# Three small moves in a one-core transformer-block kernel: a GpSimd row copy, two table tests, and the router's row

## The chip, the cores and the metric

The kernel runs on one core of a Trainium2 chip. A core has engines with an instruction queue each, and each queue runs in order: PE (TensorE, matrix products), ACT (ScalarE), DVE (VectorE), POOL (GpSimd) and SP (SyncE, which here only issues DMA transfers). A queue whose first instruction waits for a semaphore holds back everything behind it. The metric is the device time of one execution in microseconds (us); lower is better.

## The reference

One block on x of 2048 tokens by 512 features. A condition vector c gives six rows (shift, scale and gate, twice) through `silu(c) @ w_mod`. The first half is a Fourier mixing layer with DFT matrices that are handed in as inputs, the second a feed-forward network on the one token that a router picks.

```python
mod = (silu(c) @ w_mod).reshape(1, 6, 1, 512)
sa, ca, ga, sb, cb, gb = (mod[:, i] for i in range(6))
h = layernorm(x) * (1 + ca) + sa
a, b = h @ hid_re.T, h @ hid_im.T            # 512 x 512
x = x + ga * (seq_re @ a - seq_im @ b)       # 2048 x 2048 each
h = layernorm(x) * (1 + cb) + sb
r = h @ w_r                                  # a score for each token
k = argmax(r)                                # one token of 2048
y = (silu(h[k] @ w_gate) * (h[k] @ w_up)) @ w_down
x = x + gb * (h + scatter(k, y * sigmoid(r[k])))
```

## The kernel before

The two sequence matrices hold 32 MB, far more than the transform needs when they really are a cosine and a sine table. The kernel therefore takes a short path, `folded`, that computes the transform from a few columns of them, and on the way it reads all 32 MB and tests that each number is the one that the symmetry foresees. If a test fails, a flag sends the program to a long path, `general`, which does not run with these inputs.

**The tests.** The 32 MB come as 32 tiles of 128 x 2048 (1 MB each; `tst`), loaded by SP (line 600) into a ring of slots F1, R2, F2, R4, R0, R1 and R3. A slot first holds something else (R0 to R4 the weights `wm` that make the six rows, F1 and F2 the normalised input `n` of class 1) and takes its next tile when the one in it has been tested. `run_test(k)` puts the next k tests into the program at the place where it is called: six of the tests (numbers 12, 14, 16, 19, 24 and 27) are counted on VectorE (line 619, 2.3 us each), all others summed on ScalarE (line 631, 2.0 us each). A call thus decides where a test stands among an engine's other work, and with it when its slot comes free, and so where the next load can be issued by SP, which works through its list in the order of the program.

**The front.** The tokens stand in two classes of eight tiles of 128 tokens, each class in two quads: (class, quad) is (1, 0), (1, 1), (0, 0), (0, 1). The first three quads get their mean and variance by VectorE (`bn_stats`, lines 241 and 242), then four small instructions on GpSimd (lines 245 to 248) make the factor `rsa` and the shift `nma`, and ScalarE normalises the four tiles into `n` (line 276). The quad (0, 1) gets its sums from ScalarE (line 259 on) and its last steps from GpSimd (lines 269 to 272, `sst`). VectorE adds and subtracts mirrored tiles (`p`, lines 696 to 700), multiplies by the row `ca` (706) and folds (712 to 716) into `z` and `odd`. PE turns `odd` into `so` (line 792, four PSUM banks); ScalarE copies these to `xo` (line 813). PE also makes the rows of the condition: `pm_ca`, `pm_sa` (line 142), then `pq_b` and `pq_g` (line 160), whose weights lie in R3, R2, R4 and R0.

A row of 4.5 KB, `lone`, is loaded by SP into the slot `early`; its last 129 numbers are copied to `lrow` by GpSimd (line 590). `lrow` is first read in the even sequence, by the small product `sz<-lrow,lz`.

**The middle.** PE forms `h` from `xo` (line 894) for the first two pairs of token tiles, then the even sequence `st`, `sz` (line 792), then `h` of the other six pairs. VectorE adds `h` to x (282), takes the mean (290), the router's score (313), the output (334, 338); ScalarE squares (297) and makes the gains (327); GpSimd makes the factor `rs` (308, 309). SP stores each pair (353) and loads the network's weights `w_gate`, `w_up` and `w_down` (360, 363) into slots that tests and tables leave.

**The end.** `route` finds the token of the highest score: VectorE reduces to `mp`, PE turns it into one row `prow`, a copy of half of it goes to `row`, and VectorE finds the maximum (391 to 396). PE spreads the result (`pb`, `pw`, `px`), and `ffn` runs: `pg`, `pu` (467), `pd` (518), then the sum `fr` and its store of one row of the output (547), which must come after the stores of the tiles that hold this row. `keep_warm(n)` issues n products of zeros on PE; the list `WARM` has their numbers at four places of `route`, of which the first stands ahead of `prow` and the second between `prow` and `pb`.

Of the kernel before, what the change touches and what calls it, by code (L numbers as in the profile page):

```python
# [10 lines left out]
AF = mybir.ActivationFunctionType  # L11
# [3 lines left out]
P = 128  # L15
# [16 lines left out]
RD = float(D) ** 0.5  # L32
BIG = 4096.0
TOL = 2.0**-33
WARM = (44, 11, 6, 10)
EW = 4 * P + 2
SLOT = 4 * EW
SMALL = 3 * NT + NTEST + 1 + 21
# [13 lines left out]
class Path:  # L52
# [318 lines left out]
    def route(self, fill=iter(()), verdict=lambda: None):  # L371
        nc, one = self.nc, self.one
        self.keep_warm(WARM[0])
        mp = one.tile([P, 2], F32, name="mp")
        nc.gpsimd.tensor_tensor(self.nm, self.mean, self.rs, op=ALU.mult)
        nc.vector.tensor_mul(self.r, self.r, self.rs)
        nc.vector.tensor_reduce(mp[:, 0:1], self.r, axis=AX.X, op=ALU.max)
        eq = one.tile([P, NT], F32, name="eq")
        nc.vector.scalar_tensor_tensor(eq, self.r, mp[:, 0:1], self.nt, op0=ALU.is_equal, op1=ALU.mult)
        nc.vector.tensor_reduce(mp[:, 1:2], eq, axis=AX.X, op=ALU.max)  # L380
        next(fill, None)
        prow = self.ps("prow")
        for k in range(2):
            nc.tensor.matmul(
                prow[0:1, k * P : (k + 1) * P], mp[:, k : k + 1], self.ident, start=True, stop=True
            )
        self.keep_warm(WARM[1])
        row = one.tile([1, P], F32, name="row")
        nc.scalar.activation(row, prow[0:1, P : 2 * P], AF.Copy)
        fin = one.tile([1, 2], F32, name="fin")  # L390
        nc.vector.tensor_reduce(fin[:, 0:1], prow[0:1, 0:P], axis=AX.X, op=ALU.max)
        row2 = one.tile([1, P], F32, name="row2")
        nc.vector.scalar_tensor_tensor(
            row2, prow[0:1, 0:P], fin[:, 0:1], row, op0=ALU.is_equal, op1=ALU.mult
        )
        nc.vector.tensor_reduce(fin[:, 1:2], row2, axis=AX.X, op=ALU.max)
        next(fill, None)
        pb = self.ps("pb")
        nc.tensor.matmul(pb[:, 0:2], self.ones[0:1, :], fin, start=True, stop=True)
        self.keep_warm(WARM[2])  # L400
        bst = one.tile([P, 2], F32, name="bst")
        nc.vector.tensor_copy(bst, pb[:, 0:2])
        sel = one.tile([P, 5], F32, name="sel")
        for i, tab in enumerate((self.tid, self.rs, self.nm, self.rid, self.ones[:, 0:NT])):
            hit = one.tile([P, NT], F32, name=f"hit{i}")
            nc.vector.scalar_tensor_tensor(
                hit, self.nt, bst[:, 1:2], tab, op0=ALU.is_equal, op1=ALU.mult, accum_out=sel[:, i : i + 1]
            )
        pw = self.ps("pw")
        nc.tensor.matmul(pw[:, 0:4], self.ones, sel[:, 0:4], start=True, stop=True)  # L410
        self.keep_warm(WARM[3])
        ti = one.tile([1, 2], I32, name="ti")
        nc.vector.tensor_copy(ti, pw[0:1, 0:4:3])
        tj = nc.vector.value_load(ti[0:1, 0:1], min_val=0, max_val=NT - 1)
        xw = self.scrap("xw", "o")
        nc.vector.tensor_copy(xw, self.xall[:, bass.ds(tj, 1), :])
        px = self.ps("px")

        for k in range(ND):
            nc.tensor.matmul(px[:, k : k + 1], xw[:, k:D:ND], sel[:, 1:2], start=True, stop=True)  # L420
        win = one.tile([P, 2], F32, name="win")
        nc.vector.tensor_copy(win, pw[:, 1:3])
        verdict()
        xs = one.tile([P, ND], F32, name="xs")
        nc.vector.scalar_tensor_tensor(
            xs, px[:, 0:ND], win[:, 1:2], self.cbs[:, 0, :], op0=ALU.add, op1=ALU.mult
        )
        nc.vector.tensor_add(xs, xs, self.cbs[:, 1, :])
        self.xw, self.sel, self.win, self.bst, self.ti = xw, sel, win, bst, ti
        return xs  # L430
# [128 lines left out]
class Folded(Path):  # L559
# [26 lines left out]
    def load_lone(self):  # L586
        t = self.early[0:1, 4 * P :][:, 0 : 8 * P + ZC]
        self.nc.sync.dma_start(t, self.io["lone"])
        self.erow, self.v1 = t[:, 0 : 4 * P], t[:, 4 * P : 8 * P]
        self.nc.gpsimd.tensor_copy(self.lrow, t[:, 8 * P :])  # L590

    def free(self, *names):

# [314 lines left out]
    def verdict(self):  # L908
        nc, one, tot = self.nc, self.one, self.tot
        self.bad = one.tile([1, 1], I32, name="bad")  # L910
        nc.vector.tensor_reduce(tot[:, 0:1], self.esum, axis=AX.X, op=ALU.add)
        nc.vector.tensor_tensor(tot[:, 2:3], tot[:, 0:1], tot[:, 1:2], op=ALU.is_le)
        nc.vector.tensor_reduce(tot[:, 3:4], self.cnt, axis=AX.X, op=ALU.add)
        nc.vector.scalar_tensor_tensor(
            tot[:, 2:3], tot[:, 3:4], 2048.0 * len(COUNTED), tot[:, 2:3], op0=ALU.is_equal, op1=ALU.mult
        )
        self.pf = pf = self.ps("pf", "acc")
        nc.tensor.matmul(pf[0:1, 0:1], tot[:, 2:3], self.ones[:, 0:1], start=True, stop=True)
# [5 lines left out]
def folded(ctx, tc, io):  # L924
    p = Folded(ctx, tc, io)
    nc = p.nc
# [24 lines left out]
    def mirror(*at):  # L951
        pm[at] = p.mirror(*at, n[at])
# [20 lines left out]
    sums = p.statistics(0, 1, p.scalar_sums)  # L973
    stats = p.statistics(0, 0)
    last = p.scalar_statistics(*sums)
    two = p.mod_pair(wcb, wga, "b")
    p.load_wt(("R1", "R3"))
    n[0, 0] = p.normal(0, 0, stats)
# [20 lines left out]
    p.gb = p.spread_exit(p.mod_spread(other, 1, "gb"), "gb")  # L999
    for i, t in enumerate((p.cb1, p.sb)):  # L1000
        p.mod_b_columns(i, t)
    p.run_test(3)
    mirror(0, 1)
    fold(0, 1)
    p.shift_row(sa)
    p.odd_products(0, 1)
    p.run_test(1)
    p.hidden_sines(ga)
    p.hidden_turned()
    p.lone_row(n[0, 0])  # L1010
    for _ in p.odd_exits():
        pass
# [54 lines left out]
    gains(1)  # L1067
    p.run_test(2)
    p.verdict_small()
    tests = {2: 3, 3: 2, 4: 3, 5: 2, 6: 1}  # L1070
    weights = {2: 1, 3: 1, 4: 2, 5: 2, 6: 3}
    for k in range(2, late):
        begin(k)
# [98 lines left out]
@with_exitstack  # L1172
def adaln_fnet_mod_kernel(ctx: ExitStack, tc: tile.TileContext, io):
    with ExitStack() as fast:
        bad = folded(fast, tc, io)
    with tc.If(bad > 0):
        with ExitStack() as slow:
            general(slow, tc, io)
# [172 lines left out]
```

## Time and profile before

| | |
|---|---|
| time, median of 3 runs | 173.5 us (172.93 to 173.74) |
| the profiled execution: its time, its span | 172.23 us, 170.4 us |
| granted clock of PE, mean | 0.928 |
| busy: PE, DVE, ACT, POOL | 145.0, 122.2, 115.3, 29.9 us |
| moved by DMA | 62.40 MB, mean 366 GB/s |

The span runs from the first to the last instruction of one profiled execution; the time of that execution is 1.8 us longer. Times in the rows below are us from the start of the span. In the rows of the timeline the first column is the start, the second the duration (of several merged instructions where `xN` is above 1), then engine, line, operation, what is written and what is read, and in brackets the idle time of the engine before it and who ended it.

### The profile page before, as it was taken

The page shows a single profiled execution, that of the slowest core. Times are in us where ns is not written, and L with a number is a line of the kernel's source. Part 1 is how long each engine was busy: PE and PEld are TensorE (multiplying, and loading weights), DVE is VectorE, ACT ScalarE, POOL GpSimd, SP SyncE. Part 2 cuts the span into 40 slices and gives each one's busy share as a digit, 9 for nine tenths or more (in the row PEclk, how much of TensorE's full clock was granted, in tenths as well). Part 3 has the DMA queues.
Part 4 walks back from the last instruction along what each step waited for, and adds up shares of the span by engine and source line. Part 5 has one row for each costly group of instructions (what it writes and reads, how often), then busy time and mean ns, then how long its engine had stood idle before and what let it go on. Part 6 is the DMA issues. An engine that isn't in the chain of part 4 may idle for free.

```text
span 170.4 us, 2139 instructions
## 1 busy us (share of the span) xinstructions
PE 145.0 (85%) x680; PEld 69.2 (41%) x680; DVE 122.2 (72%) x256; ACT 115.3 (68%) x189; POOL 29.9 (18%) x67
## 2 busy tenths in 40 slices
PE   7999800599999942999999999999999999689970
PEld 3554300222233211444555444444444455365860
DVE  0680039997999999958779139999999973649250
ACT  3000099987969999999799999999987359400100
POOL 6000440087000002000259103042020301000000
PEclk9999965579999995799999999999999999996999
DMA  4999999501999999999999999999999999999800
GB/s 135 431 414 440 418 421 410 240 0 42 419 413 427 419 411 421 421 408 429 429 421 417 415 431 347 430 423 413 431 417 425 419 420 425 423 425 422 352 34 10
DMA packets 10108, 62.40 MB, mean 366 GB/s; under 512 B 1637, under 2 KB 1641, under 8 KB 4330
## 3 DMA queue, kind: packets, MB, share of 16 engines
q1 hardware_dynamic: 9938, 62.20, 88.8%
q8 instruction: 7, 0.11, 0.3%
q14 instruction: 11, 0.09, 0.1%
q10 hardware_dynamic: 152, 0.00, 0.1%
HBM read 57.99 MB, written 4.20 MB: 365 GB/s over the span
## 4 chain that ended last, share of the span: by engine, by line
PE 38%; DVE 28%; issue 14%; ACT 12%; POOL 5%; DVEq 1%; POOLq 0%; ACTq 0%
PE h L894 13%; ACT tst L631 5%; PE so L792 5%; DVE o L338 4%; DVE tst L619 4%; DVE xall L282 4%; DVE o L334 4%; PE sz L792 4%; DVE tv L313 4%; ACT n L276 3%; PE st L792 3%; PE pg L467 3%; PE pd L518 2%; PE pu L467 2%; POOL rsa L246 2%
## 5 line engine op out<-in xcount | busy, mean ns | idle before, releaser
L631 ACT ACTIVATE tst<-tst,small_in 128x2048 f32<-128x2048 f32 (+1 forms) x27 | 52.0, 1929 | 0.0
L792 PE MATMUL so<-eo,odd 128*128 128x512 f32 (+1 forms) x40 | 21.7, 676 | 10.8 <-DVE odd L716 10.8
L125 PE MATMUL warm<-zb 128*128 128x384 bf16 x132 | 24.9, 348 | 1.1 <-DVE zb L92 1.1
L894 PE MATMUL h<-wc,xo 128*128 128x512 f32 x32 | 16.8, 652 | 5.5 <-ACT xo L813 5.5
L276 ACT ACTIVATE n<-xall,nma,rsa 128x512 f32<-128x512 f32 x12 | 8.8, 802 | 17.5 <-POOL nma L248 17.5
L125 PEld LDWEIGHTS <-zb 128*128 128x128 bf16 x132 | 13.4, 104 | 12.2 <-issue 4.3
L792 PEld LDWEIGHTS so<-eo,odd 128*128 128x128 f32 (+1 forms) x40 | 6.6, 188 | 25.1 <-issue 13.2
L282 DVE SCALAR_TENSOR_TENSOR xall<-xall,h 128x512 f32<-128x512 f32 x16 | 10.5, 682 | 8.7 <-PE h L894 8.7
L297 ACT ACTIVATE jsq<-xall,mean 128x512 bf16<-128x512 f32 x16 | 11.5, 720 | 7.3 <-DVE mean L290 7.0
L619 DVE TENSOR_SCALAR_CACHE_REDUCE tst<-tst,small_in 128x2048 bf16<-128x2048 f32 x6 | 14.0, 2342 | 0.6 <-DMA tst<-in_tst 0.6
L308 POOL TENSOR_SCALAR rs<-ssq 128x2 f32<-128x2 f32 x8 | 3.3, 411 | 59.4 <-ACT jsq L297 59.4
L334 DVE SCALAR_TENSOR_TENSOR o<-xall,mean,n 128x512 f32<-128x512 f32 x16 | 12.0, 747 | 0.9 <-ACT n L327 0.9
L338 DVE SCALAR_TENSOR_TENSOR o<-o,mean,sb 128x512 f32<-128x512 f32 x16 | 12.0, 750 | 0.5
L313 DVE SCALAR_TENSOR_TENSOR tv<-xall,mean,vr 128x512 bf16<-128x512 f32 x16 | 12.0, 751 | 0.5
L699 DVE TENSOR_TENSOR p<-n 128x1024 f32<-128x1024 f32 x3 | 3.6, 1212 | 12.1 <-ACT n L276 12.1
L894 PEld LDWEIGHTS h<-wc,xo 128*128 128x128 f32 x32 | 6.5, 207 | 13.7 <-ACT xo L813 6.9
L894 PE MATMUL h<-wc,xe 128*128 128x512 f32 x24 | 11.3, 592 | 0.0
L327 ACT ACTIVATE n<-cb,rs 128x512 f32<-128x512 f32 x16 | 10.6, 707 | 0.1
L479 ACT ACTIVATE g<-pg 128x256 f32<-128x256 f32 (+1 forms) x2 | 0.7, 358 | 12.2 <-DVE o L334 9.6
L241 DVE BATCH_NORM_STATS2 st<-xall 128x6 f32<-128x512 f32 x12 | 8.0, 667 | 0.0
L309 POOL TENSOR_TENSOR rs<-rs,nhalf 128x2 f32<-128x2 f32 x8 | 7.5, 942 | 0.7
L894 PE MATMUL h<-wp,xo 128*128 128x512 f32 x16 | 7.5, 592 | 0.0
(210 smaller groups left out, 238.6 us busy)
## 6 DMA issues: line engine op xcount, KB each, us to landing
tst<-in_tst SPq DMA_DIRECT2D x32, 1024.0 KB, 10.7
wm<-in_wm SPq DMA_DIRECT2D x6, 1024.0 KB, 15.6
out<-o SPq DMA_DIRECT2D x8, 512.0 KB, 11.3
w_gate<-in_w_gate SPq DMA_DIRECT2D x4, 896.0 KB, 16.4
w_up<-in_w_up SPq DMA_DIRECT2D x4, 896.0 KB, 14.4
w_down<-in_w_down SPq DMA_DIRECT2D x3, 1024.0 KB, 16.2
xall<-in_x SPq DMA_DIRECT2D x1, 2048.0 KB, 14.3
wt<-in_wt SPq DMA_DIRECT2D x2, 1024.0 KB, 4.7
```

Source lines behind the costliest of these rows:

```text
L125: self.nc.tensor.matmul(dst, self.zb[:, 0:P], self.zb, start=True, stop=True)
L276: self.nc.scalar.activation(dst, src, AF.Identity, scale=rs[:, i : i + 1], bias=nm[:, i : i + 1])
L282: self.nc.vector.scalar_tensor_tensor(x, x, 1.0, y, op0=ALU.mult, op1=ALU.add, accum_out=self.sums[:, j : j + 1])
L297: self.nc.scalar.activation(junk, self.xall[:, j, :], AF.Square, bias=self.mean[:, j : j + 1], accum_out=self.ssq[:, j : j + 1],)
L313: self.nc.vector.scalar_tensor_tensor(junk, self.xall[:, j, :], self.mean[:, j : j + 1], self.vr, op0=ALU.add, op1=ALU.mult, accum_out=sel ...
L327: self.nc.scalar.activation(w[:, i, :], self.G, AF.Identity, scale=self.rs[:, j : j + 1], bias=1.0)
L334: self.nc.vector.scalar_tensor_tensor(o[:, i, :], self.xall[:, j, :], nm, w[:, i, :], op0=ALU.add, op1=ALU.mult)
L338: self.nc.vector.scalar_tensor_tensor(o[:, i, :], o[:, i, :], nm, self.sg, op0=ALU.subtract, op1=ALU.add)
L619: self.nc.vector.tensor_scalar(t.bitcast(BF16)[:, 0:2048], t, self.nref[:, i : i + 1], None, op0=ALU.is_equal, op1=ALU.add, accum_out=self ...
L631: self.nc.scalar.activation(v, v, AF.Abs, bias=self.nref[:, acc : acc + 1], accum_out=self.esum[:, acc : acc + 1])
L792: self.nc.tensor.matmul(dst, a, b, start=first and i == 0, stop=last and i == len(ops) - 1)
L894: self.nc.tensor.matmul(bank, src[:, part, dt, b, :], w[:, dt, :], start=n == 0, stop=n == 3)
```

## The change

GpSimd's copy into `lrow` leaves the function that loads the row and stands now behind the last input statistics. The third test of the call `run_test(3)` moves out, so that the tests from number 4 on come one place later each; the call `run_test(1)` that stood ahead of the sine matrices comes behind them; and the number is made up for at the stage of pair 2, which runs four tests instead of three. Since a test's number decides its engine, the six counted ones move along VectorE's list too. The router's `row` is copied by VectorE instead of ScalarE. The first two calls of `keep_warm` in `route` issue five products fewer each.

```diff
-WARM = (44, 11, 6, 10)
+WARM = (39, 6, 6, 10)
...
         row = one.tile([1, P], F32, name="row")
-        nc.scalar.activation(row, prow[0:1, P : 2 * P], AF.Copy)
+        nc.vector.tensor_copy(row, prow[0:1, P : 2 * P])
...
         self.erow, self.v1 = t[:, 0 : 4 * P], t[:, 4 * P : 8 * P]
-        self.nc.gpsimd.tensor_copy(self.lrow, t[:, 8 * P :])
+        self.late_row = t[:, 8 * P :]
...
     last = p.scalar_statistics(*sums)
+    nc.gpsimd.tensor_copy(p.lrow, p.late_row)
...
-    p.run_test(3)
+    p.run_test(2)
     mirror(0, 1)
     fold(0, 1)
     p.shift_row(sa)
     p.odd_products(0, 1)
-    p.run_test(1)
     p.hidden_sines(ga)
     p.hidden_turned()
+    p.run_test(1)
     p.lone_row(n[0, 0])
...
-    tests = {2: 3, 3: 2, 4: 3, 5: 2, 6: 1}
+    tests = {2: 4, 3: 2, 4: 3, 5: 2, 6: 1}
```

GpSimd's list in the front of the program, before; the first `rsa` and `nma` are those of quad (1, 0), the second those of (1, 1):

```order
L584 MEMSET early 1x128 x4
L590 COPY lrow<-early 1x129
L245 TENSOR_SCALAR rsa_211<-mv_202 128x4
L246 TENSOR_TENSOR rsa_211<-rsa_211,nhalf 128x4
L247 TENSOR_TENSOR nma_212<-mv_202,rsa_211 128x4
L248 TENSOR_SCALAR nma_212<-nma_212 128x4
L245 TENSOR_SCALAR rsa_232<-mv_223 128x4
```

and after, from the third statistics on (their first line is the quad (0, 0), `sst` is (0, 1)):

```order
L248 TENSOR_SCALAR nma_232<-nma_232 128x4
L245 TENSOR_SCALAR rsa_335<-mv_326 128x4
L246 TENSOR_TENSOR rsa_335<-rsa_335,nhalf 128x4
L247 TENSOR_TENSOR nma_336<-mv_326,rsa_335 128x4
L248 TENSOR_SCALAR nma_336<-nma_336 128x4
L269 TENSOR_SCALAR sst_306<-sst_305 128x4
L270 TENSOR_TENSOR sst_306<-sst_306,nhalf 128x4
L271 TENSOR_SCALAR sst_306<-sst_306 128x4
L272 TENSOR_TENSOR sst_307<-sst_304,sst_306 128x4
L976 COPY lrow<-early 1x129
L878 MEMSET eh 1x2x512
```

The copy was the first instruction of GpSimd to read something loaded, ahead of all statistics; now all sixteen instructions of the statistics stand ahead of it.

ScalarE's list between the row `gb` and the first `xo`, before:

```order
L182 ACTIVATE gb<-pm_gb 128x512
L631 ACTIVATE tst_424,esum<-tst_424,small_in 128x2048
L631 ACTIVATE tst_426,esum<-tst_426,small_in 128x2048
L631 ACTIVATE tst_428,esum<-tst_428,small_in 128x2048
L631 ACTIVATE tst_431,esum<-tst_431,small_in 128x2048
L868 ACTIVATE wn<-wp,sgn 128x512
L869 ACTIVATE wn<-wp 128x512
L813 ACTIVATE xo<-so_295 128x512
```

and after:

```order
L182 ACTIVATE gb<-pm_gb 128x512
L631 ACTIVATE tst_424,esum<-tst_424,small_in 128x2048
L631 ACTIVATE tst_426,esum<-tst_426,small_in 128x2048
L868 ACTIVATE wn<-wp,sgn 128x512
L869 ACTIVATE wn<-wp 128x512
L631 ACTIVATE tst_428,esum<-tst_428,small_in 128x2048
L813 ACTIVATE xo<-so_294 128x512
```

Four tests stood ahead of the first `xo`, three do now, and one of these three stands behind the matrix `wn`.

VectorE's list around the even sequence, where counted tests (L619) move; before, from the scores of pair 0 to the sum of pair 2:

```order
L313 SCALAR_TENSOR_TENSOR tv_577,r<-xall,mean,vr 128x512
L619 TENSOR_SCALAR tst_538,cnt<-tst_538,small_in 128x2048
L282 SCALAR_TENSOR_TENSOR xall,sums<-xall,h_584 128x512
...
L619 TENSOR_SCALAR tst_543,cnt<-tst_543,small_in 128x2048
L334 SCALAR_TENSOR_TENSOR o_667<-xall,mean,n_8_620 128x512
...
L619 TENSOR_SCALAR tst_550,cnt<-tst_550,small_in 128x2048
L901 TENSOR_TENSOR cke<-small_in 128x5
```

and after:

```order
L313 SCALAR_TENSOR_TENSOR tv_574,r<-xall,mean,vr 128x512
L282 SCALAR_TENSOR_TENSOR xall,sums<-xall,h_581 128x512
...
L619 TENSOR_SCALAR tst_538,cnt<-tst_538,small_in 128x2048
L334 SCALAR_TENSOR_TENSOR o_664<-xall,mean,n_8_617 128x512
...
L619 TENSOR_SCALAR tst_544,cnt<-tst_544,small_in 128x2048
L619 TENSOR_SCALAR tst_550,cnt<-tst_550,small_in 128x2048
L901 TENSOR_TENSOR cke<-small_in 128x5
```

Test 12 (`tst_538`) no longer stands ahead of the sum of pair 1, and test 16 (`tst_550`) follows test 14 directly, ahead of the sum of pair 2.

## The prediction

> **What bounds the kernel now.** I read the page's busy shares and its 40 slices first, because a share is an average over stages with different limits.
>
> ```profile
> PE 145.0 (85%) x680; PEld 69.2 (41%) x680; DVE 122.2 (72%) x256; ACT 115.3 (68%) x189; POOL 29.9 (18%) x67
> ...
> DMA  4999999501999999999999999999999999999800
> ```
>
> A slice is 4.26 us. The DMA engines are full nearly everywhere, with one hole in the slices 8 to 10, some 32 to 42 us. Windows laid over it give its size (the last three columns are PE's granted clock, DMA's share and GB/s):
>
> ```profile
> 32.00:36.00 4.00, 4.00 (x6) 1.35 (x5) 3.83 (x9) 3.81 (x12) 1.24 (x2) 0.50 0.07 25
> 36.00:40.00 4.00, 4.00 (x18) 0.80 (x20) 3.96 (x5) 2.24 (x5) 3.68 (x4) 0.93 0.00 0
> 40.00:44.00 4.00, 3.48 (x27) 0.87 (x19) 3.05 (x6) 4.00 (x7) 1.82 (x3) 1.00 0.52 180
> 44.00:100.00 56.00, 50.47 (x131) 22.16 (x131) 45.77 (x82) 52.66 (x82) 8.63 (x17) 0.94 1.01 421
> 100.00:108.00 8.00, 8.00 (x20) 3.52 (x19) 6.58 (x12) 7.96 (x13) 1.68 (x2) 1.00 1.01 386
> ```
>
> Against the 421 GB/s of the long window, the first three lack 4.00 x (1 - 25/421) = 3.76, 4.00 and 4.00 x (1 - 180/421) = 2.29 us: **10.05 us** of transfers. So there is a stream of transfers that stops once and then hardly pauses, and beside it a chain of work. Who makes the hole is told by SP's timeline:
>
> ```profile
> 18.93 22.11 SPq L233 DMA_DIRECT2D wt<-in_wt  x2
> 41.14 15.89 SPq L600 DMA_DIRECT2D tst<-in_tst  x7
> ```
>
> The second `wt` is held until 41 us: it needs slot R3, which PE must have read for `pq_b`, and PE's list has the products of `odd` ahead of that. `odd` goes back to GpSimd, in order of time:
>
> ```profile
> 8.68 0.18 DVE L242 BATCH_NORM_AGGREGATE mv<-st 128x2 f32<-128x6 f32 x1
> ...
> 19.04 0.28 POOL L590 COPY lrow<-early 1x129 f32<-1x129 f32 x1 [15.41 <-DMA early<-in_lone]
> 19.29 0.23 POOL L245 TENSOR_SCALAR rsa<-mv 128x4 f32<-128x4 f32 x1
> ...
> 21.00 0.25 POOL L248 TENSOR_SCALAR nma<-nma 128x4 f32<-128x4 f32 x1
> 21.29 2.93 ACT L276 ACTIVATE n<-xall,nma,rsa 128x512 f32<-128x512 f32 x4 [15.81 <-POOL nma L248]
> ...
> 24.24 1.23 DVE L699 TENSOR_TENSOR p<-n 128x1024 f32<-128x1024 f32 x1 [12.12 <-ACT n L276]
> ...
> 30.70 0.69 DVE L716 TENSOR_TENSOR odd<-z 128x513 f32<-128x513 f32 x1
> ```
>
> The means of quad (1, 0) are there at 8.86. GpSimd takes them up at 19.29, since the copy ahead of them waits for a row that lands at 19.04. ScalarE and VectorE stand idle for 15.8 and 12.1 us.
>
> **The front.** Without the copy, the four instructions start at about 8.9 and last 1.96 (19.29 to 21.25): `n` starts at 10.9 instead of 21.29, 10.4 earlier. What is late next? First `ca`, whose product is
>
> ```profile
> 11.47 3.67 PE L142 MATMUL pm_ca<-wm,sc 128*128 128x512 f32 x8
> ```
>
> done at 15.14. VectorE has `n` at 13.85, and its first two instructions (L699 and L700, 1.23 each) fill the time to 16.4; `ca` is there by then. From the start of L699 to the end of `odd` are 7.15 us (24.24 to 31.39): `odd` at 21.0, **-10.35**. Next come the loads of class 0 (issued at 5.26) and of the last `wm` (issued at 15.2):
>
> ```profile
> xall<-in_x SPq DMA_DIRECT2D x1, 2048.0 KB, 14.3
> wm<-in_wm SPq DMA_DIRECT2D x1, 1024.0 KB, 14.3
> 42.92 1.10 PE L177 MATMUL pm_cb<-pair_b,early 128*128 128x512 f32 x2 [0.52 <-ACT pair_b L172]
> ```
>
> They land at 19.6, ahead of VectorE's wish at 21.0, and at 29.5. PE wants the second for `pq_g` at about 28 and waits, but then needs 2 us for it, and `pm_cb`, the next in its list, would start at 42.92 - 10.35 = 32.6 anyway. The shift of 10.35 stays.
>
> GpSimd's price is not certain, for these instructions now run beside VectorE. The same four beside VectorE's work with two operands,
>
> ```profile
> 34.68 1.11 POOL L245 TENSOR_SCALAR rsa<-mv 128x4 f32<-128x4 f32 x1 [11.38 <-DVE mv L242]
> ...
> 38.24 1.08 POOL L248 TENSOR_SCALAR nma<-nma 128x4 f32<-128x4 f32 x1
> ```
>
> take 4.64 (34.68 to 39.32) instead of 1.96. The bounds are 0 and +2.7. Beside the moved ones VectorE runs `bn_stats`, with one operand; the nearest row of that kind is a small GpSimd instruction beside a counted test:
>
> ```profile
> 118.06 0.22 POOL L308 TENSOR_SCALAR rs<-ssq 128x2 f32<-128x2 f32 x1 [3.47 <-ACT jsq L297]
> ```
>
> It is as short as L245 alone (0.23), so I take 0 and keep 2.7 for the range.
>
> The Trainium skill speaks to this ("SBUF — State Buffer", "Who interferes with whom"): a VectorE instruction with two SBUF inputs contends with a GpSimd instruction that reads SBUF, one with at most one input outside the two-port modes does not. By that rule the price is 0 as well; the two rows agree with it, though none has `bn_stats` and GpSimd side by side.
>
> The moved copy (0.28 alone; four times that by the ratio of L245's rows) stands behind `sst`. Its row has long landed, and behind it in GpSimd's list comes a memset that waits for VectorE far into the program. It costs nothing.
>
> **The stream.** With `odd` at 21.0, its products take 5 to 7 us, `pq_b` is done by 30, and the second `wt` is issued while the transfers issued before still run (they fill the time to 32). The hole closes: -10.05. But the loads of tests hang on ScalarE: a load is issued when the test that had its slot is done. Loads 9 and 10 follow tests 4 and 5, which come 1.3 us (behind `wn`) and 3.2 us (behind `xo`) later against the rest of the program. For load 10 that leaves some 5.5 us from issue to the time at which the stream would bring it. A lone load takes 4.7:
>
> ```profile
> wt<-in_wt SPq DMA_DIRECT2D x1, 1024.0 KB, 4.7
> ```
>
> So I charge +0.5 (bounds 0 and 2) and have **-9.55**. On SP one store (pair 0) comes a place earlier, ahead of a load; the stream is the same in sum.
>
> **The tests.** Ahead of the first `h` stand, in the timeline:
>
> ```profile
> 56.88 4.82 PE L792 MATMUL so<-eo,odd 128*128 128x512 f32 x10
> ...
> 63.49 1.99 ACT L631 ACTIVATE tst<-tst,small_in 128x2048 f32<-128x2048 f32 x1
> ...
> 66.60 2.03 ACT L813 ACTIVATE xo<-so 128x512 f32<-128x512 f32 x4
> 67.23 3.67 PE L894 MATMUL h<-wc,xo 128*128 128x512 f32 x4 [5.53 <-ACT xo L813]
> ```
>
> One test of four goes: **-2.0** (1.99). `so` is done at 61.7, five us before `xo` wants it: no hindrance. From there PE runs without a pause to 101, then VectorE to 138 (busy 35.95 of 37):
>
> ```profile
> 67.00:101.00 34.00, 33.77 (x94) 16.75 (x95) 23.58 (x49) 32.64 (x53) 7.69 (x16) 0.95 1.01 420
> 101.00:138.00 37.00, 37.00 (x98) 16.70 (x97) 35.95 (x73) 30.10 (x46) 7.08 (x10) 1.00 1.01 414
> ```
>
> What moves must not lengthen these two. The waits that can take it in are
>
> ```profile
> DVE xall L282 <- PE h L894: 8.7, 4, 3.4
> ACT jsq L297 <- DVE mean L290: 7.0, 4, 4.2
> ```
>
> (total us, times, longest). On VectorE tests 14 and 16 (2.3 us each) and the gains, which come 2 us late, fall where it waits for `h` before pair 2. On ScalarE the extra test at pair 2 makes it 2 us late, and its four waits for VectorE's mean make that good. If the cover fails, it costs up to 2.
>
> **The router.**
>
> ```profile
> 135.37 7.31 PE L125 MATMUL warm<-zb 128*128 128x384 bf16 x44
> ...
> 141.81 0.17 DVE L380 TENSOR_REDUCE mp<-eq 128x1 f32<-128x16 f32 x1
> 141.90 0.74 DVE L334 SCALAR_TENSOR_TENSOR o<-xall,mean,n 128x512 f32<-128x512 f32 x1
> 142.61 0.60 PE L384 MATMUL prow<-ident,mp 128*1 128x128 f32 x4
> ...
> 145.65 0.28 DVE L391 TENSOR_REDUCE fin<-prow 1x1 f32<-1x128 f32 x1 [3.01 <-ACT row L389]
> ```
>
> VectorE waits 3.01 us because ScalarE has the last two tests ahead of `row`. Five products of zeros fewer (5 x 7.31/44 = 0.8) let `prow` start at 142.0, when `mp` is there; it ends at 142.6, as does L334. The copy on VectorE is a read of the same 128 numbers as L391; I take its 0.28. `fin` starts at 142.95: **-2.7**. The second group of zeros, six now (1.0), is done before `pb` is wanted at 144.
>
> **The sum.** The chain of work comes 10.35 + 2.0 + 2.7 = 15.05 earlier. But the last store, of the router's row, waits for the stores of the tiles too:
>
> ```profile
> L547 ACTq EVENT_SEMAPHORE  x3: 38/38/38, 162.1 to 163.4; - x3
> L547 ACTq DMA_DIRECT2D out<-fr x1: 1136/1136/1136, 166.0 to 166.0; - x1
> ```
>
> These waits end at 163.4, and the store goes out at 166.0, when `fr` is ready. After the change `fr` would be ready at 150.9 by its own chain, but the tiles' stores, at the end of the stream, land at 163.4 - 9.55 = 153.85. The store goes out at 153.9 instead of 166.0: **-12.1**. So 3 us of the chain's gain are not seen. Span 158.3; this execution's time 172.23 - 12.1 = 160.1. The median of the runs shown is 1.27 above this execution, so 173.5 - 12.1 = **161.4 us**.
>
> **Rivals.** (1) The stream loses still less: load 10 comes in time (0.5), and dips like that to 386 GB/s at 100 to 108 (8 x 35/421 = 0.7) and others of its size vanish with the earlier chain. Then about 14 are gained: 159.6. (2) The front pays: GpSimd takes 2.7 more, `odd` comes at 23.7, PE's clock has fallen by then, and loads of tests run dry by 2 us. Of 10.05 there are 6 to 9 left: 162.5 to 166. (3) The second `wt` or the first slots are late by another wait, and half of the hole stays: 168.5. The landings above speak against it. (4) The copy isn't what holds `rsa`, and another wait ends at 19 as well. Of the chain's 4.7 us the stores let 2.5 through: 171. In GpSimd's new list `rsa` waits for VectorE and GpSimd alone, which speaks against it. (5) **Slower**, by PE's clock: the work of 67 to 101 is 33.8 us of PE at 0.95. With other pauses ahead of it, PE could be granted half the clock there; each us of full-speed work then costs one more. From 12 us of such work on the gain is gone; if the whole stage stays at half, the time is 161.4 + 32 = 193. Against it: after the longest pause of PE the clock was 0.50 at 32 to 36 and 0.93 at 36 to 40 again.
>
> A rule of the Trainium skill would expect little of this change: "Perfetto Trace Analysis", "Identifying the Most-Contended Engine", has the engine of the highest occupancy optimized first, and GpSimd has 18%. By it the outcome would be that of rival 4. The trace bears out the remark that follows there, on regimes that change over time: in the first 21 us it is GpSimd that all others wait for.
>
> **How the numbers follow.** Forecast 0.60; (1) 0.12; (2) 0.20; (3) 0.03; (4) 0.02; (5) 0.03. The range takes in (1) and (2): 159 to 166. A measurement of this kernel can tell about 0.5% from no change. All but (5) are faster by more than that, with a hundredth left for less: 0.96, 0.01, 0.03.
>
> **What would show it.** `n` of quad (1, 0) at about 11; no pause of the transfers between 30 and 45; `xo` at about 54.3; `fin` without a wait for ScalarE, at about 130.6 (142.95 less 10.35 and 2.0); the last store held by the tiles' stores instead of `fr`. I am wrong if the hole is still there, if ScalarE's tests wait for their loads one after the other, or if PE is at half clock between 55 and 89.

## The result, and the profile after

| | before | after |
|---|---|---|
| median, first comparison | 173.22 us (172.41 to 173.74, 4 runs) | 160.62 us (159.93 to 162.25, 4 runs) |
| ratio, first comparison | | 0.929 [0.921, 0.937] |
| median, second comparison | 173.65 us (171.97 to 174.41, 11 runs) | 159.94 us (159.73 to 160.19, 6 runs) |
| ratio, second comparison | | 0.923 [0.918, 0.927] |
| the profiled execution: its time, its span | 172.23, 170.4 us | 159.93, 158.1 us |

Medians and ranges here and below take in every run, the ratios leave out the few slow ones, which lie more than 1.5% above the fastest of their kernel.

The forecast was 161.4 us (159 to 166). Between the two profiled executions of the first comparison lie 12.3 us; 12.1 were forecast. The numbers after the change come from this execution, unless the second comparison is named.

The page of after, busy times and the two slice rows that answer to those of before (a slice is now 3.95 us):

```profile
PE 141.8 (90%) x670; PEld 67.1 (42%) x670; DVE 121.8 (77%) x257; ACT 114.7 (73%) x188; POOL 29.0 (18%) x67
...
PEclk9999999999999999999999999999999999995997
DMA  4999999999999999999999999999999999999940
```

The engines are busy nearly as long as before (PE 3.2 us less), and the hole of the transfers is gone. The windows of after, laid over the place of the hole and on to 80 us (last columns: PE's granted clock, DMA share, GB/s):

```profile
32.00:36.00 4.00, 4.00 (x11) 1.27 (x8) 3.84 (x4) 4.00 (x8) 0.00 (x0) 1.00 1.02 426
36.00:40.00 4.00, 4.00 (x10) 1.26 (x9) 3.83 (x7) 3.10 (x8) 0.00 (x0) 1.00 1.01 416
40.00:44.00 4.00, 4.00 (x11) 1.18 (x9) 3.97 (x5) 3.23 (x5) 0.00 (x0) 1.00 1.02 428
44.00:56.00 12.00, 8.39 (x19) 2.93 (x20) 11.43 (x22) 11.64 (x16) 0.94 (x1) 1.00 1.02 418
56.00:68.00 12.00, 12.00 (x29) 5.30 (x28) 10.74 (x28) 12.00 (x12) 0.00 (x0) 1.00 0.99 384
68.00:80.00 12.00, 11.86 (x47) 6.86 (x46) 7.42 (x13) 11.81 (x25) 4.16 (x8) 1.00 1.01 426
```

All three windows of the old hole are full. One dip is left, 384 GB/s in 56 to 68; against 421 it costs 12 x 37/421 = 1.05 us.

The front, in the timeline of after:

```profile
8.65 0.18 DVE L242 BATCH_NORM_AGGREGATE mv<-st 128x2 f32<-128x6 f32 x1
8.80 0.69 DVE L241 BATCH_NORM_STATS2 st<-xall 128x6 f32<-128x512 f32 x1
8.99 0.24 POOL L245 TENSOR_SCALAR rsa<-mv 128x4 f32<-128x4 f32 x1 [5.37 <-DVE mv L242]
...
10.72 0.25 POOL L248 TENSOR_SCALAR nma<-nma 128x4 f32<-128x4 f32 x1
11.01 2.93 ACT L276 ACTIVATE n<-xall,nma,rsa 128x512 f32<-128x512 f32 x4 [5.57 <-POOL nma L248]
13.97 1.22 DVE L699 TENSOR_TENSOR p<-n 128x1024 f32<-128x1024 f32 x1 [1.88 <-ACT n L276]
20.42 0.69 DVE L716 TENSOR_TENSOR odd<-z 128x513 f32<-128x513 f32 x1
...
31.66 0.28 POOL L976 COPY lrow<-early 1x129 f32<-1x129 f32 x1
```

GpSimd now waits for VectorE's means and for nothing else. `odd` starts at 20.42 instead of 30.70, 10.28 earlier. The middle, with the group of the first products of `h` (busy time, mean ns of one) behind its first instruction:

```profile
54.39 2.03 ACT L813 ACTIVATE xo<-so 128x512 f32<-128x512 f32 x4
55.02 1.98 PE L894 MATMUL h<-wc,xo 128*128 128x512 f32 x4 [3.61 <-ACT xo L813]
...
L894 PE MATMUL h<-wc,xo 128*128 128x512 f32 x32 | 15.1, 595 | 3.6 <-ACT xo L813 3.6
```

The first four products of `h` took 3.67 before. The router and the end of the timeline, then the instructions of line 547 (shortest, median and longest duration in ns, then the first and the last start):

```profile
128.89 0.27 DVE L389 COPY row<-prow 1x128 f32<-1x128 f32 x1
129.09 0.27 DVE L391 TENSOR_REDUCE fin<-prow 1x1 f32<-1x128 f32 x1
136.48 1.93 PE L467 MATMUL pg<-w_gate,xs 128*32 128x256 f32 x32 [0.39 <-DVE xs L428]
142.12 3.18 PE L467 MATMUL pu<-w_up,xs 128*32 128x256 f32 x25 [1.56 <-DMA w_up<-in_w_up]
153.32 0.29 DVE L546 TENSOR_TENSOR fr<-fr,tk 128x128 f32<-128x128 f32 x1
...
L547 ACTq EVENT_SEMAPHORE  x4: 17/38/38, 148.4 to 154.4; - x4
L547 ACTq DMA_DIRECT2D out<-fr x1: 1136/1136/1136, 154.6 to 154.6; - x1
```

`fr` is ready at 153.6, and the store goes out at 154.6, when the waits for the tiles' stores have ended. The chain is late itself by then because `pu` waits for its weights, 2.7 us in two waits (1.11 and 1.56), and its 25 products then take 3.18 us at a granted clock of 0.50 (143 to 145); in the profiled execution of the second comparison they took 1.70 behind a wait of 1.02. So what sets the end is the stream of transfers, once directly and once through `w_up`.

### The profile page after: what moved, and what is told of

Read it like the earlier page. It is cut to its first block, busy times and chain, and to the rows that moved or that the text cites. A ratio compares the mean times of both kernels' runs of the same rounds, so it can differ in the third digit from the quotient of the medians.

```text
span 158.1 us, 2117 instructions
## 1 busy us (share of the span) xinstructions
PE 141.8 (90%) x670; PEld 67.1 (42%) x670; DVE 121.8 (77%) x257; ACT 114.7 (73%) x188; POOL 29.0 (18%) x67
## 4 chain that ended last, share of the span: by engine, by line
DMA 44%; ACT 27%; PE 19%; issue 5%; SPq 1%; DVE 0%
ACT tst L631 17%; DMA wm<-in_wm 16%; DMA out<-o 10%; DMA w_up<-in_w_up 10%; DMA tst<-in_tst 9%; PE so L792 6%; PE pu L467 3%; ACT jsq L297 3%; PE pm_ca L142 2%; PE pd L518 2%; ACT n L327 2%; PE pq_g L160 1%; ACT eh L882 1%; PE pg L467 1%; ACT xo L813 1%
## 5 line engine op out<-in xcount | busy, mean ns | idle before, releaser
L125 PE MATMUL warm<-zb 128*128 128x384 bf16 x122 | 23.2, 349 | 1.1 <-DVE zb L92 1.1
L792 PE MATMUL so<-eo,odd 128*128 128x512 f32 (+1 forms) x40 | 19.2, 608 | 0.6 <-DVE odd L716 0.6
L894 PE MATMUL h<-wc,xo 128*128 128x512 f32 x32 | 15.1, 595 | 3.6 <-ACT xo L813 3.6
L125 PEld LDWEIGHTS <-zb 128*128 128x128 bf16 x122 | 12.4, 105 | 11.5 <-issue 4.3
L619 DVE TENSOR_SCALAR_CACHE_REDUCE tst<-tst,small_in 128x2048 bf16<-128x2048 f32 x6 | 14.0, 2340 | 0.0
L308 POOL TENSOR_SCALAR rs<-ssq 128x2 f32<-128x2 f32 x8 | 2.3, 288 | 57.0 <-ACT jsq L297 57.0
L792 PEld LDWEIGHTS so<-eo,odd 128*128 128x128 f32 (+1 forms) x40 | 5.8, 167 | 13.1 <-issue 11.8
L894 PEld LDWEIGHTS h<-wc,xo 128*128 128x128 f32 x32 | 6.0, 190 | 11.2 <-issue 6.5
L467 PE MATMUL pu<-w_up,xs 128*32 128x256 f32 (+1 forms) x64 | 6.3, 458 | 2.7 <-DMA w_up<-in_w_up 2.7
## 6 DMA issues: line engine op xcount, KB each, us to landing
w_gate<-in_w_gate SPq DMA_DIRECT2D x4, 896.0 KB, 16.8
```

The costliest lines, as they stand in the source:

```text
L125: self.nc.tensor.matmul(dst, self.zb[:, 0:P], self.zb, start=True, stop=True)
L467: nc.tensor.matmul(dst[32 * j : 32 * (j + 1), :], xs[:, k : k + 1].to_broadcast([P, 32]), wsb[j][:, k, a * FA[0] : a * FA[0] + FA[a]], sta ...
L619: self.nc.vector.tensor_scalar(t.bitcast(BF16)[:, 0:2048], t, self.nref[:, i : i + 1], None, op0=ALU.is_equal, op1=ALU.add, accum_out=self ...
L792: self.nc.tensor.matmul(dst, a, b, start=first and i == 0, stop=last and i == len(ops) - 1)
L894: self.nc.tensor.matmul(bank, src[:, part, dt, b, :], w[:, dt, :], start=n == 0, stop=n == 3)
```

## The experiments

**One part at a time.** Four kernels ran together with the kernel before (173.68 us, 13 runs). First the copy's move alone, put into the kernel before:

```diff
-        self.nc.gpsimd.tensor_copy(self.lrow, t[:, 8 * P :])
+        self.late_row = t[:, 8 * P :]
...
     last = p.scalar_statistics(*sums)
+    nc.gpsimd.tensor_copy(p.lrow, p.late_row)
```

> Only GpSimd's copy moves; tests, router and warming products stay as before. Theory (a stream of transfers and a chain of work, of which the later one ends the kernel): the stream's hole of 10.05 us closes, and the chain comes 10.35 earlier, some 1.5 more if PE's clock no longer falls ahead of h; the chain is then the later of the two, and the time is 10.4 to 11.9 below before: 161.3 to 162.8. Rival A (the tests and the router bring a good part of the 12.6): 164 to 167. Rival B (the copy is not what holds the statistics): no change, 173.

162.9 us (161.88 to 163.51), ratio 0.939 [0.932, 0.945]: 10.8 of the 12.6 us, 0.1 above the range of the theory, and rivals A and B fall. In its profiled execution, the slowest of the four, the chain is the later of the two, as expected, but by 0.4 us only: the waits for the tiles' stores end at 156.8, and the store goes out at 157.2, when `fr` is ready.

```profile
L547 ACTq EVENT_SEMAPHORE  x3: 38/38/38, 154.9 to 156.8; - x3
L547 ACTq DMA_DIRECT2D out<-fr x1: 1135/1135/1135, 157.2 to 157.2; - x1
```

The same edit taken out of the kernel after leaves the tests and the router alone:

```diff
-        self.late_row = t[:, 8 * P :]
+        self.nc.gpsimd.tensor_copy(self.lrow, t[:, 8 * P :])
...
-    nc.gpsimd.tensor_copy(p.lrow, p.late_row)
```

> The copy stays where it was before; the tests, the router's row and the warming products are as after the change. Theory: the chain comes 4.7 earlier, the stream stays, and the last store still waits for the tiles' stores at about 163.4 in the span: at most 2.5 below before, 170.7 to 171.5. Rival A: 4 to 5 below before, 168.5. Rival C (the later tests starve the stream): 173 or above.

171.9 us (170.59 to 173.47), ratio 0.992 [0.988, 0.996]. The instructions of line 547 in this kernel say why its shorter chain is worth only 1.8 us:

```profile
L547 ACTq EVENT_SEMAPHORE  x4: 17/38/38, 156.9 to 165.1; - x4
L547 ACTq DMA_DIRECT2D out<-fr x1: 1136/1136/1136, 165.2 to 165.2; - x1
```

ScalarE's queue reached the first of these waits at 156.9 and was held there to 165.1 by the tiles' stores. With the hole still in it, the stream ends no earlier. In this execution its last waits even end 1.7 us later than before (165.1 against 163.4), and the median lies 0.4 above the range of the theory; what makes these stores later is not shown.

Then the kernel after with the tests back at their old places (3, 1 and 3 tests in the three calls):

```diff
-    p.run_test(2)
+    p.run_test(3)
...
-    tests = {2: 4, 3: 2, 4: 3, 5: 2, 6: 1}
+    tests = {2: 3, 3: 2, 4: 3, 5: 2, 6: 1}
```

> After the change, with the tests back in their old places. Theory: the chain comes 10.35 + 2.7 earlier (and the clock's 1.5 where it holds), the stream 10.05 without the 0.5 to 1 that the later loads cost; both end within a us of each other, so 160 to 161.5, the same as after the change or a little faster. Rival D (the two later tests are needed, since xo waits for them): 162.5 to 163.

161.06 us (160.25 to 162.06), ratio 0.930 [0.923, 0.938]; the last store went out at 155.9, just behind the tiles' stores at 155.8. And the kernel after with the router's row on ScalarE and the old numbers of zeros:

```diff
-WARM = (39, 6, 6, 10)
+WARM = (44, 11, 6, 10)
...
-        nc.vector.tensor_copy(row, prow[0:1, P : 2 * P])
+        nc.scalar.activation(row, prow[0:1, P : 2 * P], AF.Copy)
```

> After the change, with the router's row back on ScalarE and the old counts of warming products. Theory: the chain loses 2.7, but has some us in hand against the stream, since the products with w_up wait for it: 160.6 to 162, within 1% of after the change. Rival E (the router's 2.7 us are on the path that sets the end): 163.3.

161.0 us (160.21 to 162.84), ratio 0.930 [0.921, 0.938]. Its first row below, from the router's line 391, shows that the wait of 3 us which the router's edit removes is there again; the others show that it costs nothing at the end:

```profile
  ACT row L389: 3.0, 1
...
L547 ACTq EVENT_SEMAPHORE  x4: 17/38/38, 148.6 to 153.8; - x4
L547 ACTq DMA_DIRECT2D out<-fr x1: 1135/1135/1135, 153.9 to 153.9; - x1
```

By the medians, each of the last two edits is worth 1.8 to 1.9 us on top of the move alone, and the other then adds nothing that these runs can tell apart (ratios to before of 0.930 and 0.930 against 0.929 and 0.923).

**A smaller dose of the wait.** In the kernel before, the load of the row is issued earlier, and the copy keeps its place ahead of all statistics:

```diff
     p.load_columns()
+    p.load_lone()
     p.odd_columns()
     wsa = p.load_wm(0, "R1")
     p.load_x(0)
-    p.load_lone()
```

> Before, with the load of the row lone issued right behind the first two quads of x instead of behind the class-0 loads' place; the copy still stands ahead of all statistics in GpSimd's list. A dose test of the wait. Theory (it is the wait for the row's landing that holds the front): lone lands at about 12, the copy ends then, n of quad (1, 0) starts at about 14.6 instead of 21.3, 6.7 us earlier; the hole of the transfers at 32 to 42 shrinks to about 3 us or less, time 166 to 168. Rival (the copy instruction itself, or another wait that ends at 19, costs the time): n stays at 21, time 173.5.

165.29 us (164.57 to 166.94) against 172.86 for the kernel before, ratio 0.959 [0.950, 0.967]. The copy and the first `n` in its timeline, and the windows of the hole:

```profile
11.71 0.28 POOL L590 COPY lrow<-early 1x129 f32<-1x129 f32 x1 [8.09 <-DMA early<-in_lone]
...
13.96 2.92 ACT L276 ACTIVATE n<-xall,nma,rsa 128x512 f32<-128x512 f32 x4 [8.63 <-POOL nma L248]
...
32.00:36.00 4.00, 3.65 (x33) 1.08 (x26) 3.05 (x6) 3.96 (x6) 2.34 (x4) 1.00 0.46 125
36.00:40.00 4.00, 4.00 (x9) 1.05 (x8) 3.96 (x5) 4.00 (x9) 0.00 (x0) 1.00 1.01 414
```

The row lands 7.3 us earlier (11.71 against 19.04), `n` starts 7.3 us earlier, the hole shrinks to 4 x (1 - 125/421) = 2.8 us, and the time falls by 7.6. That is somewhat more than expected, as the row came sooner than 12. Between the profiled executions, 165.30 and 172.23 us, it is 6.9. So it is the wait for the row, not the copy and not another wait, and its effect runs through to the end nearly us for us. Rival 4 falls.

**The clock of PE ahead of `h`.** The kernel before, with products of zeros where PE waits for `xo`:

```diff
+    def keep_warm_ps(self, n):
+        dst = self.ps("warmh")[:, 0:384]
+        for _ in range(n):
+            self.nc.tensor.matmul(dst, self.zb[:, 0:P], self.zb, start=True, stop=True)
...
     p.odd_products(0, 1)
+    p.keep_warm_ps(27)
     p.run_test(1)
```

> Before, with 27 products of zeros on PE between the products of odd and the first h, where PE idles for 5.5 us ahead of xo. Theory (part of what the change gained ahead of h is PE's clock: in the kernel before the first h ran at half clock after the pause, 3.67 us for four products, and in the kernel after at full clock, 1.98): the first four products take about 2.0, the products of h in all 15.1 instead of 16.8 us, and the time is 1.5 to 1.7 us less, about 172. Rival (h's stage is paced by what takes h from the banks, not by PE): h shortens but the time stays within 0.5 of 173.5.

170.83 us (169.34 to 173.69) against 172.86, ratio 0.986 [0.981, 0.991]. The first products and their group (its line numbers are 5 higher):

```profile
67.36 1.98 PE L899 MATMUL h<-wc,xo 128*128 128x512 f32 x4 [1.15 <-ACT xo L818]
...
L899 PE MATMUL h<-wc,xo 128*128 128x512 f32 x32 | 15.1, 595 | 1.2 <-ACT xo L818 1.2
```

The group shrinks from 16.8 to 15.1 us and the time by 2.0 (1.3 between the profiled executions, 170.89 and 172.23). In the kernel before, PE's clock was on the path.

**The stream against the chain.** The kernel after without the last four tests:

```diff
+LOADED = 28
...
-        while self.next_load < NTEST and TEST_AT[self.next_load] in self.empty:
+        while self.next_load < LOADED and TEST_AT[self.next_load] in self.empty:
...
-        for i in range(self.next_run, min(self.next_run + n, NTEST)):
+        for i in range(self.next_run, min(self.next_run + n, LOADED)):
```

> After, with the last four tests (28 to 31) neither loaded nor run: 4.2 MB of transfers less, that is 9.96 us of the stream at 421 GB/s; that part of the check of the sequence matrices is left out. Theory (the stream of transfers sets the end of the kernel after, the chain only waits for it): pu no longer waits for w_up, the tiles' stores end before fr is ready, the last store goes out at about 148 to 149 when fr is ready, span about 152.5, time about 154. Rival (the chain sets the end): the last store stays at about 153 to 154.6, time 160 to 160.6.

155.07 us (154.44 to 159.71, one of the four runs above 156), ratio 0.898 [0.890, 0.905]. The end of its timeline (its lines are 1 higher):

```profile
147.88 0.29 DVE L547 TENSOR_TENSOR fr<-fr,tk 128x128 f32<-128x128 f32 x1
...
148.20 1.14 ACTq L548 DMA_DIRECT2D out<-fr  x1
```

No wait of `pu` for `w_up` is left among PE's waits, and the store goes out as soon as `fr` is there. The tests left out were work of ScalarE too, but that is not what made the chain shorter: `fin` is at 129.07 here and at 129.09 in the kernel after. So the chain of the kernel after alone, with PE's clock as in that execution, would have its last store at 148.2, and for 154.6 - 148.2 = 6.4 us it is held by the transfers.

**Where the stream still loses.** In the dip at 56 to 68, load 10 waits for a slot. The next kernel changes the list of slots, so that loads 10 and 11 go to R1 and R3, which are free earlier:

```diff
-TEST_AT = (RING * 2 + RING[:2] + ["R1", "R3", "F2", "R4", "R0", "F1", "R2"] * 3)[:NTEST]
-FFN_AT = ["F5", "F7", "F6", "F8", "F3", "R2", "R1", "R3", "F2", "R4", "R0", "F4"]
+TEST_AT = RING * 2 + (["R1", "R3"] + RING) * 3 + ["F1"]
+FFN_AT = ["F5", "F7", "F6", "F8", "F3", "R1", "R3", "R2", "F2", "R4", "R0", "F4"]
```

It ran with the kernel after, with a kernel that has 12 products of zeros in PE's wait for the last `wm`, and with one that has both:

```diff
     two = p.mod_pair(wcb, wga, "b")
+    p.keep_warm_ps(12)
     p.load_wt(("R1", "R3"))
```

> The changed kernel itself, unedited, as the reference for the three kernels that run on the same chip with it. Every theory: 160.6, within 159.9 to 162.3, and the median of its profiled windows 56 to 68 us near 384 GB/s.

> After, with 12 products of zeros on PE between the second condition matrix (pair_b) and pq_g, where PE waits for the last wm. Theory (in some executions PE's granted clock falls to half in this pause, and the products of odd that follow then take up to 1.65 us longer, as in the run that moved the copy alone): clock 1.00 at 28 to 36 us in every execution, odd's products 4.8 us, the first test on ScalarE at 41.9; the time is 0 to 1 us below the kernel after run beside it, and its spread smaller. Rival (the end is set by the tiles' stores at the end of the stream, so the front's clock is not seen): within 0.4 us of the kernel after.

> After, with loads 9 to 11 of the tests handed to other slots: the slots R1 and R3, free at about 53.5 us, take loads 10 and 11 instead of the slots that wait for tests 5 and 6. Theory (the stream loses about 1.05 us in the window 56 to 68 because too few loads are outstanding there): that window rises from 384 to about 420 GB/s, the tiles' stores land 1 us earlier, time about 159.7. Rival (the window is low for another cause, such as the mix of stores and loads, or what is won is lost in the next dip): window below 400 GB/s or time unchanged within 0.4 us.

> After, with both edits: the slots R1 and R3 for loads 10 and 11, and the 12 products of zeros. If the two theories hold, the window 56 to 68 is near 420 GB/s, the clock does not fall at 28 to 36, and the time is 159.2 to 159.8. If only the stream counts, it equals the kernel with the slots alone; if neither counts, 160.6.

| | median | ratio to before |
|---|---|---|
| after | 159.94 us (159.73 to 160.19) | 0.923 [0.918, 0.927] |
| zeros | 160.15 us (159.42 to 162.34) | 0.924 [0.918, 0.929] |
| slots | 158.78 us (158.55 to 159.77) | 0.918 [0.913, 0.923] |
| both | 158.59 us (158.20 to 158.68) | 0.915 [0.911, 0.920] |

SP's timeline of the kernel after and ScalarE's beside it show what load 10 waited for:

```profile
54.51 4.25 SPq L600 DMA_DIRECT2D tst<-in_tst  x2
...
56.30 2.01 ACT L631 ACTIVATE tst<-tst,small_in 128x2048 f32<-128x2048 f32 x1
58.20 0.21 ACT L631 ACTIVATION_READ_ACCUMULATOR tst<-tst,small_in 128x1 f32 x1
```

SP is held with the second of these two loads until test 5 has ended at 58.4. With other slots the window and the last waits are, in the kernel with the slots alone:

```profile
56.00:68.00 12.00, 12.00 (x23) 5.06 (x22) 10.35 (x26) 12.00 (x13) 0.00 (x0) 0.79 1.01 422
...
L547 ACTq EVENT_SEMAPHORE  x4: 17/38/38, 147.3 to 153.0; - x4
```

The dip is gone (422 GB/s), the tiles' stores release the last store at 153.0 instead of 154.4, and 1.2 us are gained. The times with the slots lie below the expected ones, as the kernel after itself ran at 159.94 instead of the 160.6 that they started from. The zeros alone gain nothing, and their spread is wider than that of the kernel after, not smaller. The windows at 28 to 36 of the kernel after (in the second comparison) and of the one with zeros:

```profile
28.00:36.00 8.00, 6.28 (x23) 1.80 (x24) 7.02 (x10) 7.60 (x13) 3.64 (x6) 1.00 1.02 420
28.00:36.00 8.00, 7.99 (x35) 2.82 (x34) 7.02 (x10) 7.60 (x13) 3.63 (x6) 1.00 1.02 420
```

PE is busy for 7.99 of 8 us instead of 6.28, but the clock was 1.00 already: there was nothing to cure in this execution, and the stream sets the end in any case. The version with both is the fastest that does all of the work, 158.59 / 159.94 = 0.992 of the kernel after on the same chip. Whether the zeros add to the slots stays open: the medians differ by 0.2 us. Two of the six runs with the slots alone took 159.8 us, and none with both took more than 158.7, but no profile of those two runs is there.

## Why the prediction was right, step by step

- **What bounds the kernel: right.** A wait in the list of an engine that is busy for 18% of the span held everything else; the smaller dose shows it by itself.
- **The front, -10.35: right.** `odd` came 10.28 earlier. GpSimd's price, bounded by 0 and +2.7, is 0: the four instructions took 1.98 us (8.99 to 10.97) beside `bn_stats`, against 1.96 alone. The Trainium skill ("SBUF — State Buffer", "Who interferes with whom") has it that a VectorE instruction with at most one SBUF input, outside the two-port modes, does not contend with GpSimd. The rows of after have the two side by side and agree: L245 took 0.24 us beside `bn_stats`. The first part of rival 2 falls.
- **The stream, -9.55: nearly right.** The hole closed whole. The charge for load 10 was mis-sized: +0.5 was taken (bounds 0 and 2), the dip at that place costs 1.05, and the change of slots confirms that a load waits for its slot there, and about the size. The last waits for the tiles' stores moved by 163.4 - 154.4 = 9.0. That the moved tests cause the dip, as the prediction has it, is not shown. The windows of after, of the copy's move alone and of the kernel with the tests back at their old places, in this order, are alike at the same place:

```profile
48.00:72.00 24.00, 20.39 (x53) 9.20 (x52) 21.22 (x48) 23.97 (x31) 1.09 (x2) 1.00 1.01 402
48.00:72.00 24.00, 18.34 (x39) 7.32 (x39) 18.95 (x39) 23.64 (x30) 0.94 (x1) 0.93 0.99 389
48.00:72.00 24.00, 18.35 (x39) 7.40 (x38) 19.75 (x39) 23.64 (x29) 0.94 (x1) 0.93 0.99 396
```

  In the last two executions, though, `pq_g` ran at half clock and the first test began 1.6 us later than in the kernel after, so they do not clear the moved tests either.
- **The chain, -15.05: too small in one execution, right in another.** The sum of the chain took every duration as it stood before; what it left out is PE's clock, which the same kernel can keep or lose. In the execution shown above the products of `h` lost 1.7 us (16.8 to 15.1), and `fin` came at 129.09 instead of 130.6: 16.56 earlier. Then `pg` took 1.93 us; its row of before has 3.44:

```profile
152.88 3.44 PE L467 MATMUL pg<-w_gate,xs 128*32 128x256 f32 x32 [0.44 <-issue]
```

  With both, `fr`'s store would be due at 166.0 - 16.56 - 1.51 = 147.9; the kernel without the last four tests has it at 148.2. The profiled execution of the second comparison is the same kernel with the clock lost at both places:

```profile
130.56 0.27 DVE L391 TENSOR_REDUCE fin<-prow 1x1 f32<-1x128 f32 x1
...
L467 PE MATMUL pg<-w_gate,xs 128*32 128x256 f32 x32 | 3.4, 603 | 0.4 <-DVE xs L428 0.4
L547 ACTq EVENT_SEMAPHORE  x4: 17/38/38, 147.3 to 154.4; - x4
```

  Here `fin` came 15.09 earlier, as forecast, `pg` took 3.4 us as before, and by the same sum `fr`'s store would be due at 150.9. The waits for the tiles' stores end at 154.4 in both, and the two executions took 159.93 and 159.88 us. So PE's clock is luck for the chain, and no longer counts for the time.
- **Tests and router, -2.0 and -2.7: there, but covered.** The waits went as foretold (`xo` 12.21 earlier, 12.35 forecast; `fin` without its wait). But either edit alone brings as much as both. In the profiled executions with one of them the two ends lie close: `fr` is ready at 153.9 and the waits end at 153.8 with the router's row on ScalarE, 154.5 and 155.8 with the tests at their old places.
- **The last store, held by the tiles' stores: right.** 154.6 instead of 153.9, by the mis-sized charge of the stream.
- **The span: right by two errors that cancel.** The store was 0.7 us later than forecast, and what lies behind it was shorter: 170.4 - 166.0 = 4.4 us before, 158.1 - 154.6 = 3.5 after. The median was also forecast 1.27 above the profiled execution, as before the change; it was 0.7 above in the first comparison.

The surplus of the chain, 3 us in the prediction, is 6.4 us in one execution and 3.7 in the other (154.6 - 150.9). More surplus changes the time no more than those three did, which is why a chain forecast up to 3 us too long left the time nearly untouched.

The medians, 160.62 and 159.94, lie between the forecast and rival 1 (159.6). Rival 1 is right that the old dip goes (80 to 150 ran at 421 GB/s), but load 10 did not come in time, and the dip at 56 to 68 takes it back. Rivals 3 and 5 did not come about. Two prices of rivals leave out the step that the forecast itself took, that the last store went out 2.6 us behind the waits: with 6 to 9 us of the hole left to gain, rival 2 comes to 161.9 to 164.9 instead of 162.5 to 166, and with half of the hole rival 3 comes to 165.9 instead of 168.5.

## What to carry to other kernels

In an engine that runs its list in order, look at the wait of the first instruction that reads a load, not at how busy the engine is: a copy of 0.28 us held the whole front for 10 us. Another place for it cures all of that, an earlier load 7.3 us. Make the sum twice, once for the chain of work and once for the stream of transfers, and take the later of the two: what shortens the other one is free cover, not gain. When the stream sets the end, the next gain is a slot for a load that waits, here 1.2 us for a changed list.

## What was not expected of the hardware

**A pause of PE doesn't always cost its clock.** Where PE waits 3.5 to 3.6 us for `xo`, the products of `h` that follow took 15.1 us in two profiled executions and 15.9 to 16.9 in the six others with that wait; behind 5.5 to 5.7 us they took 16.7 to 16.9 in all four. The kernel after itself has both, in two executions:

```profile
55.02 1.98 PE L894 MATMUL h<-wc,xo 128*128 128x512 f32 x4 [3.61 <-ACT xo L813]
55.01 2.77 PE L894 MATMUL h<-wc,xo 128*128 128x512 f32 x4 [3.56 <-ACT xo L813]
```

A shorter pause can cost it too: with the copy's move alone, `pq_g` came after waits of 0.39 and 1.45 us and ran at half clock,

```profile
30.82 3.38 PE L160 MATMUL pq_g<-wm,sc 128*32 128x512 f32 x12 [1.45 <-DMA wm<-in_wm]
32.00:33.00 1.00, 1.00 (x6) 0.19 (x2) 0.89 (x1) 1.00 (x2) 0.00 (x0) 0.50 0.97 401
```

and with the tests at their old places it did so again (3.40 us), while in the kernel after the same instructions, after the same waits, took 1.91. The first `pg` shows the like: behind 0.39 to 0.44 us of idle time its 32 products took 1.93 us in three profiled executions and 2.84 to 3.54 in the ten others. The Trainium skill ("TensorE: Matmul & The Clock Gate", "HAM oscillation — how this bites in real kernels") puts the bound at idle gaps above about 3.4 us. The gaps of 5.5 us and more agree with it; the gaps of 3.5 to 3.6 us lie above it and kept the clock twice; the gaps of 1.45 us and less lie below it and lost it in two kernels ahead of `pq_g` and in ten ahead of `pg`. Why is not shown here. A forecast should therefore carry both prices for such a place.

**What lies behind the last store has two lengths.** It is 4.4 us where `fr` comes last and 3.5 us where the tiles' stores do: 161.6 - 157.2 with the copy's move alone and 158.3 - 153.9 with the router's row on ScalarE, but 168.7 - 165.2 without the move and 156.7 - 153.1 with the other slots. All thirteen profiled executions fall into these two kinds, within 0.1 us. Where the 0.9 us go is not shown.
